# PSUM banks in a 4-2-2 and a 3-2-3 division, in an attention kernel with a fast-product MLP mixer behind it

## The chip, the cores and the metric

The kernel runs on one core of a Trainium2 chip. The metric is the device time of one execution in microseconds (us), as the median of several runs. The core's engines are TensorE (PE), VectorE (DVE), ScalarE (ACT), GpSimd (POOL) and SyncE (SP, which issues most transfers). Each works through its own queue in order. TensorE writes its products into PSUM, which has eight banks; VectorE and ScalarE read them out, which the text calls eviction. A bank can be written again when its last reader is done.

## What is computed

Attention with normalised queries and keys over 8 batches, 12 heads, 448 positions and a head size of 64, and then an MLP mixer (token and channel) on the result, all in float32:

```python
q_n, k_n = (rmsnorm(q, g_q), rmsnorm(k, g_k))
scores = scale * np.matmul(q_n, k_n.transpose(0, 1, 3, 2))
scores = scores - np.max(scores, axis=-1, keepdims=True)
attn = np.exp(scores)
attn = attn / (np.sum(attn, axis=-1, keepdims=True) + 1e-09)
x = np.matmul(attn, v)            # then (B, H, S, D) -> (B, S, H*D)

xt = x.transpose(0, 2, 1)
h = np.maximum(xt @ w_tok1, 0.0) @ w_tok2
u = x + h.transpose(0, 2, 1)
h2 = np.maximum(u @ w_ch1, 0.0) @ w_ch2
out = u + h2
```

The sizes of the mixer are 448 positions, 768 channels, 256 for `w_tok1` and 1536 for `w_ch1`.

## The kernel before

**Overlap of two halves.** The mixer of batch b and the attention of batch b+1 run at the same time: their operations stand interleaved in each engine's queue, in an order that the Python code writes out for TensorE, VectorE, ScalarE and GpSimd (`manual_schedule`). SP's queue is ordered by the framework. From batch 2 on the two channel products of the mixer, `ch1` (line 968) and `ch2` (line 1037), use a fast matrix product: 15 block products in place of 18, whose operands are sums of blocks. Such sums are made on VectorE and GpSimd, and each product is then added into several places, by VectorE, GpSimd and ScalarE, as the tables `C1_STEPS` and `C_STEPS` say. `ch1(b, f, o)` is called 30 times a batch and `ch2(b, f, x)` 30 times; each call is four matmuls, which the profile shows as eight instructions, since a float32 matmul takes two. This text calls such a call a product. A `ch1` call takes a PSUM bank of its own; two `ch2` calls share one.

**Attention.** Pairs of heads are numbered p, and two pairs make a group t. A group has seven key blocks k. `score(t, k)` (line 433) takes two score banks, fills them with four 64x64-tiled matmuls, and ScalarE writes their exponentials into a tile `e`. `values(ps, k)` (line 503) multiplies exponentials by v and adds them up in two output banks (`ps_O`), which are held from k = 0 to k = 6. `group_sums` (line 477) adds exponentials up over k on VectorE, `row_sums` (line 522) sums them over the keys with two products with ones, one for each pair, and `denominators` (line 528) divides: `begin` reads a row-sum bank, `end` multiplies the output bank by the reciprocals (line 560) and so frees it.

**Queries and keys of the next group.** `square` (line 1363, ScalarE) squares them, `reduce` (line 1377, VectorE) sums the squares, `fold` and `guess` prepare a first reciprocal root, three `newton` steps (line 1413, four GpSimd operations each) refine it, `scale` (line 399, VectorE) multiplies, `turn_qk` (line 405) transposes on VectorE and multiplies the queries by the gains on ScalarE. Only then are the buffers free for the loads of the next group. One tile of squares serves both pairs, so `square(n+1)` waits for `reduce(n)`.

**The order around the change.** For batches 2 to 6, `big_step(t, second)` (line 570) makes two TensorE blocks of a group: the first has scores 0 to 2 of this group, values 4 to 6 of the last and its row sums, the second has scores 3 to 6 and values 0 to 3. It returns what runs ahead of the block, the block, what comes directly behind it (`beside`) and a list for the products up to the next block (`between`). Six such blocks, second and first in turn, stand before products 0, 9, 16, 25, 33 and 40 of the 60 (`BLOCKS`, line 1190). `place` (line 620) deals the list out: after the m-th of n products, `upto = -(-len(rest) * (m + 1) // n)` items of it have been emitted (line 627). In earlier batches `att_step` (line 639) makes four smaller steps of a group, merged with the other work by estimated durations.

**PSUM.** Three pools share the eight banks, and each gives its banks out in turn: `ps_S` (4) for scores, row sums, transposes, two of the token products and every other product of `ch1` and `ch2` (`c_ps`), `ps_O` (2) for the values, `ps_M` (2) for the rest (`m_ps`).

Of the kernel before, what the change touches and what calls it, by code (L numbers as in the profile page):

```python
# [110 lines left out]
def whole(ctx, tc, shifted, pre, q, k, v, g_q, g_k, moe_w_tok1, moe_w_tok2, moe_w_ch1, moe_w_ch2, out):  # L111
# [53 lines left out]
    ps_S = pool("ps_S", 4, space=PSUM)  # L165
    ps_O = pool("ps_O", 2, space=PSUM)
    ps_M = pool("ps_M", 2, space=PSUM)
# [354 lines left out]
    def row_sums(t):  # L522
        es = st.pop(("es", t))
        for p in (2 * t, 2 * t + 1):
            st["d", p] = s_tile("d_ps")
            ones(p, es[:, p % 2, :], start=True, stop=True)
# [43 lines left out]
    def big_step(t, second):  # L570
# [68 lines left out]
    def att_step(g):  # L639
# [8 lines left out]
        def finish():  # L648
            if s == 0 and t:
                last = (p - 2, p - 1)  # L650
                for k in (NK - 2, NK - 1):
                    values(last, k)
            if live:
                for k in ((0,), (1, 2), (3, 4), (5, 6))[s]:
                    score(t, k)
            if s == 0 and t:
                if not on_pe(p - 1):
                    row_sums(t - 1)
                for i in last:
                    st.pop(("v", i))  # L660

        def tiled():
# [8 lines left out]
            if inside:  # L671
                for fn in turns:
                    fn()
            if live and s and not shifted:
                for k in ((), (0,), (1, 2), (3, 4))[s]:
                    values(pair, k)
# [291 lines left out]
    def ch1(b, f, o):  # L968

        put_off_done()  # L970
        ps = m_tile() if o else s_tile("c_ps")
# [534 lines left out]
```

## Time and profile before

| | |
|---|---|
| median of 3 runs | 1314.67 us (1314.24 to 1315.56) |
| the profiled execution | 1318.08 us |
| its span, first to last instruction | 1316.2 us |
| granted TensorE clock, mean | 0.992 of full speed |
| DMA traffic | 225.60 MB, mean 171 GB/s |
| TensorE waits put down by name | t_ps for DVE at the start 15.1 us; m_ps of ch2 for DVE 9.4 (5 times); c_ps of ch1 for ACT 3.8 (3 times); m_ps of tok2 for DVE 2.9; c_ps of ch2 for ACT 2.0 (3 times) |

Stages, by TensorE's timeline in us from the span's start: attention of batch 0 from 18 to 81, batch 0's mixer to 258, batch 1's to 427, then batches 2 to 7, which begin at 426.6, 587.7, 741.5, 895.1, 1048.5 and 1196.3. Batch 7 has no attention beside it.

A line of a timeline has the start, the time from the first start to the last end, the engine, the line of the code, the operation, what it writes and reads, the shape and the number of instructions; in brackets stands idle time of the engine ahead of it and what ended it. Matmuls overlap, so their rate is read from the distance of their starts, not from the length of one. A line of a table of windows has the stretch, its length, and for each engine the busy time and the number of instructions, then the granted clock, the busy share of the DMA engines and GB/s.

### The profile page before, as it was taken

The numbers are of one execution on the slowest core, as the hardware profiler recorded it, in microseconds if no ns is written. First come the engines' busy times: TensorE is split into PE (matmuls) and PEld (weight loads), VectorE is DVE, ScalarE is ACT, GpSimd is POOL, SyncE is SP. The second block draws the span as 40 slices with busy tenths as digits, with TensorE's granted clock in tenths as the row PEclk, the third lists the DMA queues.
The fourth block names the chain that finished last, engine by engine and source line by source line (L and its number), as shares of the span: only waits on it lengthen the run. The fifth ranks groups of instructions, "written<-read, shape, count | busy, mean of one in ns | idle before, by whom it ended". The sixth has DMA issues, their size and how long they took to land.

```text
span 1316.2 us, 19628 instructions
## 1 busy us (share of the span) xinstructions
PE 1262.6 (96%) x7048; PEld 871.8 (66%) x7048; DVE 835.9 (64%) x1280; ACT 403.5 (31%) x775; POOL 469.0 (36%) x727
## 2 busy tenths in 40 slices
PE   5999999999999997999999999999999999999996
PEld 3444444444445675696777777786876967797996
DVE  6998769654463566755768368765677557664343
ACT  6663433123320243402443044321434024300210
POOL 1300100079975785430343203450234303430242
PEclk9999999999999999999999999999999999999998
DMA  9666456898888977596567766495765965476664
GB/s 210 172 178 162 120 139 169 203 259 236 234 202 230 212 210 183 114 247 123 115 174 157 191 144 148 115 232 139 167 153 113 252 122 129 122 183 157 177 178 82
DMA packets 480272, 225.60 MB, mean 171 GB/s; under 512 B 375204, under 2 KB 441764, under 8 KB 480164
## 3 DMA queue, kind: packets, MB, share of 16 engines
q1 hardware_dynamic: 462690, 206.68, 65.2%
q0 software_dynamic: 4480, 15.73, 3.9%
q10 hardware_dynamic: 12994, 1.84, 0.9%
q8 instruction: 58, 0.95, 0.3%
q14 instruction: 50, 0.41, 0.1%
HBM read 178.36 MB, written 45.81 MB: 170 GB/s over the span
## 4 chain that ended last, share of the span: by engine, by line
PE 77%; DVE 10%; DMA 4%; SPq 3%; POOL 2%; issue 2%; ACT 2%; DVEq 0%; ACTq 0%; POOLq 0%
PE m_ps L1047 12%; PE c_ps L1047 10%; PE s_ps L441 8%; PE c_ps L979 8%; PE m_ps L979 7%; PE o_ps L514 7%; PE m_ps L862 5%; PE m_ps L1010 4%; PE m_ps L935 4%; PE m_ps L1030 4%; PE t_ps L820 2%; PE m_ps L820 2%; DVE es L482 2%; DMA qk_t<-in_k_dram 2%; DVE hb L1021 1%
## 5 line engine op out<-in xcount | busy, mean ns | idle before, releaser
L445 ACT ACTIVATE e<-s_ps 128x448 f32<-128x448 f32 x294 | 141.4, 556 | 178.9 <-PE s_ps L441 168.9
L441 PE MATMUL s_ps<-qkT 64*64 64x448 f32 x1260 | 169.0, 547 | 2.5 <-DVE r L992 1.7
L1047 PE MATMUL m_ps<-hb,unit 128*128 128x224 f32 x768 | 160.4, 364 | 9.4 <-DVE r L992 9.4
L1047 PEld LDWEIGHTS m_ps<-hb,unit 128*128 128x128 f32 x768 | 150.3, 197 | 12.5 <-DVE r L992 11.1
L295 POOL TENSOR_TENSOR raw<-raw 128x128 f32<-128x128 f32 x256 | 135.2, 549 | 45.8 <-DMA out_dram<-turned 25.5
L514 PE MATMUL o_ps<-e,v 64*64 64x448 f32 x1148 | 144.8, 539 | 0.7 <-DVE uT L560 0.4
L1047 PE MATMUL c_ps<-hb,unit 128*128 128x224 f32 x672 | 135.8, 354 | 2.6 <-ACT e L445 2.0
L1047 PEld LDWEIGHTS c_ps<-hb,unit 128*128 128x128 f32 x672 | 126.3, 190 | 9.9 <-ACT e L445 4.3
L482 DVE TENSOR_TENSOR es<-es,e 128x896 f32<-128x896 f32 x90 | 105.7, 1175 | 14.6 <-ACT e L445 9.6
L441 PEld LDWEIGHTS s_ps<-qkT 64*64 64x64 f32 x1260 | 52.6, 132 | 84.1 <-issue 57.5
L979 PE MATMUL c_ps<-tu,unit 128*128 128x224 f32 x480 | 101.5, 354 | 3.9 <-ACT e L445 3.8
L979 PE MATMUL m_ps<-tu,unit 128*128 128x224 f32 x480 | 102.1, 356 | 1.7 <-DVE hb L992 1.7
L979 PEld LDWEIGHTS m_ps<-tu,unit 128*128 128x128 f32 x480 | 89.7, 190 | 9.9 <-issue 5.6
L979 PEld LDWEIGHTS c_ps<-tu,unit 128*128 128x128 f32 x480 | 90.1, 190 | 9.2 <-ACT e L445 7.6
L514 PEld LDWEIGHTS o_ps<-e,v 64*64 64x64 f32 x1148 | 52.7, 133 | 60.5 <-issue 48.0
L992 POOL TENSOR_TENSOR hb<-hb,r 128x448 f32<-128x448 f32 x36 | 49.5, 1401 | 117.6 <-DVE r L992 80.0
L1062 POOL TENSOR_TENSOR uT<-uT,r 128x448 f32<-128x448 f32 x42 | 52.5, 1262 | 104.0 <-DVE r L1062 92.0
L403 DVE TENSOR_TENSOR qk_t<-qk_t,rs 128x896 f32<-128x896 f32 (+1 forms) x42 | 55.6, 1361 | 43.5 <-POOL rs L1421 43.5
L961 POOL TENSOR_TENSOR tu<-uT 128x448 f32<-128x448 f32 x12 | 13.7, 1139 | 194.2 <-DVE uT L867 117.2
L862 PE MATMUL m_ps<-w_sb,h 128*128 128x448 f32 x192 | 74.4, 541 | 2.9 <-DVE uT L867 2.9
L1418 POOL TENSOR_TENSOR nt<-rs 128x56 f32<-128x56 f32 (+1 forms) x57 | 17.8, 313 | 160.2 <-DVE rs L1410 158.2
L1388 DVE TENSOR_REDUCE ms<-sq 128x28 f32<-128x896 f32 (+2 forms) x44 | 47.4, 1079 | 41.4 <-ACT sq L1374 38.3
(151 smaller groups left out, 1995.5 us busy)
## 6 DMA issues: line engine op xcount, KB each, us to landing
unit<-ws SPq DMA_DIRECT2D x240, 384.0 KB, 3.9
raw<-in_moe_w_ch_dram SPq DMA_DIRECT2D x72, 256.0 KB, 3.4
v<-in_v_dram SPq DMA_DIRECT2D x96, 112.0 KB, 3.9
xs<-xt SPq DMA_DIRECT2D x56, 168.0 KB, 4.5
out_dram<-turned SPq DMA_DIRECT2D x168, 56.0 KB, 2.0
unit<-wp SPq DMA_DIRECT2D x24, 384.0 KB, 4.7
ws<-raw POOLq DMA_DIRECT2D x16, 512.0 KB, 4.9
qk_t<-in_q_dram SPq DMA_DIRECT2D x144, 56.0 KB, 3.5
```

The source lines that it names most:

```text
L295: nc.gpsimd.tensor_tensor(out=at[o], in0=at[x], in1=at[y], op=ALU.add if op == "+" else ALU.subtract)
L403: nc.vector.tensor_tensor(out=x, in0=x, in1=r.unsqueeze(2).to_broadcast(list(x.shape)), op=ALU.mult)
L441: nc.tensor.matmul(out=pss[i][rows_of(i, a), 0:S], lhsT=qkT[h, 1, k * D:(k + 1) * D], rhs=qkT[h, 0, :], start=True, stop=True)
L445: nc.scalar.activation(out=e[:, i, :], in_=pss[i][:, 0:S], func=AF.Exp)
L482: nc.vector.tensor_tensor(out=es[:], in0=(es if k > 1 else st["e", t, 0])[:], in1=st["e", t, k][:], op=ALU.add)
L514: nc.tensor.matmul(out=st["o", p][a * D:(a + 1) * D, 0:S], lhsT=vt[rows, k * D:(k + 1) * D], rhs=e[rows, :], **kw)
L820: nc.tensor.matmul(out=st["t1", h][jc][:, 0:HC], lhsT=w1_sb[:, c, jc * P:(jc + 1) * P], rhs=st["x", b, h][:, :, c, :], start=start and c = ...
L862: nc.tensor.matmul(out=ps[:, 0:S], lhsT=st["h1", jc][:, cc * P:(cc + 1) * P], rhs=w2_sb[:, jc].rearrange("p c r -> p (c r)"), start=(jc == ...
L935: nc.tensor.matmul(out=ps, lhsT=a[:, o + 2 * half, :], rhs=natural(half * KF + t) if wide else u[:, half * KC + t, :], start=(t == 0 and h ...
L979: nc.tensor.matmul(out=ps[:, t * HS:(t + 1) * HS], lhsT=st["w"][:, tile_at % 6, :], rhs=x[:, k, :], start=(k == 0), stop=(k == 1))
L1010: nc.tensor.matmul(out=ps, lhsT=w[:, 3 * o + t, :], rhs=u[:, half * KC + t, :], start=(half == 0 and t == 0), stop=(half == 1 and t == KC ...
L1047: nc.tensor.matmul(out=ps[:, x * HS:(x + 1) * HS], lhsT=st["w"][:, tile_at % 6, :], rhs=hb[:, X_SLOT[f], i, :], start=(i == 0), stop=(i == 3))
```

## The change

The banks are divided 3 for `ps_S`, 2 for `ps_O` and 3 for `ps_M`. All `ch1` and `ch2` products take `ps_M`. In the blocks of `big_step` a value step follows each score step. In `att_step` the two alternate as well, with the transposes of the next queries and keys between them in batch 0's attention, and of the two row-sum banks the first comes from `ps_M`. `reduce(n+1)`, the second sum of squares, moves from directly behind the first block to after the first group sum of the list.

```diff
-    ps_S = pool("ps_S", 4, space=PSUM)
+    ps_S = pool("ps_S", 3, space=PSUM)
     ps_O = pool("ps_O", 2, space=PSUM)
-    ps_M = pool("ps_M", 2, space=PSUM)
+    ps_M = pool("ps_M", 3, space=PSUM)
...
-    def row_sums(t):
+    def row_sums(t, mixed=False):
         es = st.pop(("es", t))
         for p in (2 * t, 2 * t + 1):
-            st["d", p] = s_tile("d_ps")
+            st["d", p] = m_tile() if mixed and p % 2 == 0 else s_tile("d_ps")
             ones(p, es[:, p % 2, :], start=True, stop=True)
...
         def first_block():
-            if live:
-                score(t, 0)
-                score(t, 1)
-            if more and t > BIG:
-                pre.reduce(n, st)
-                pre.square(n + 1, st)
-            for k in range(NK - 2 - (t > BIG), NK):
-                values(last, k)
+            ks = range(NK - 2 - (t > BIG), NK)
+            for i in range(3):
+                if live:
+                    score(t, i)
+                if more and t > BIG and i == 1:
+                    pre.reduce(n, st)
+                    pre.square(n + 1, st)
+                if i < len(ks):
+                    values(last, ks[i])
             row_sums(t - 1)
             for i in last:
                 st.pop(("v", i))
-            if live:
-                score(t, 2)
 
         def second_block():
-            score(t, 3)
-            score(t, 4)
-            for k in range(4):
-                values(pair, k)
-            score(t, 5)
-            score(t, 6)
+            for k, vs in ((3, (0,)), (4, (1, 2)), (5, (3,)), (6, ())):
+                score(t, k)
+                for v in vs:
+                    values(pair, v)
...
-            ahead, beside = (squares[:1], squares[3:]) if t > BIG else ([], [])
+            ahead, beside = squares[:1] if t > BIG else [], []
             between = [item(group_sums, t, k) for k in (1, 2) if live]
+            if t > BIG:
+                between[1:1] = squares[3:]
...
         def finish():
...
+            ks = ((0,), (1, 2), (3, 4), (5, 6))[s] if live else ()
+            vs = ((NK - 2, NK - 1) if t else (), (0,), (1, 2), (3, 4))[s] if s == 0 or live else ()
+            todo = [lambda k=k: score(t, k) for k in ks]
+            of = (p - 2, p - 1) if s == 0 else pair
+            vals = [lambda k=k: values(of, k) for k in vs]
+            order = []
+            while todo or vals:
+                for l in (vals, todo) if s == 0 else (todo, vals):
+                    if l:
+                        order.append(l.pop(0))
+            between = list(turns) if inside else []
+            for fn in order:
+                fn()
+                if between:
+                    between.pop(0)()
+            for fn in between:
+                fn()
             if s == 0 and t:
                 if not on_pe(p - 1):
-                    row_sums(t - 1)
+                    row_sums(t - 1, True)
...
     def ch1(b, f, o):
...
-        ps = m_tile() if o else s_tile("c_ps")
+        ps = m_tile()
...
     def ch2(b, f, x):
...
         if x == 0:
-            st["m"] = s_tile("c_ps") if f % 2 else m_tile()
+            st["m"] = m_tile()
```

More of the change, by code (lines that the diff above doesn't have):

```diff
@@ L648, in finish @@
         def finish():
[L649 to L655, printed above, removed]
+            ks = ((0,), (1, 2), (3, 4), (5, 6))[s] if live else ()
[15 more added lines that the diff above has]
+                fn()
             if s == 0 and t:
                 if not on_pe(p - 1):
-                    row_sums(t - 1)
-                for i in last:
+                    row_sums(t - 1, True)
+                for i in last_pair:
                     st.pop(("v", i))
+        last_pair = (p - 2, p - 1)
         def tiled():
@@ L670, in tiled @@
                     st.pop(("qkT", i))
-            if inside:
+            if inside and shifted:
                 for fn in turns:
                     fn()
-            if live and s and not shifted:
-                for k in ((), (0,), (1, 2), (3, 4))[s]:
-                    values(pair, k)
         def both_shifted():
```

## The prediction

> **What bounds the kernel now.** I read the page first, then TensorE's instructions in order of time, then what VectorE, GpSimd and ScalarE do around TensorE's gaps, and last the granted clock around them.
>
> ```profile
> PE 1262.6 (96%) x7048; PEld 871.8 (66%) x7048; DVE 835.9 (64%) x1280; ACT 403.5 (31%) x775; POOL 469.0 (36%) x727
> ```
>
> TensorE is busy 96% of the span, and the change adds and removes no instruction. So only the gaps in TensorE's stream can pay or cost. I follow batch 4 (741.5 to 895.1 us); batches 3 and 5 repeat it. A to F are its six attention blocks, before mixing products 0, 9, 16, 25, 33 and 40. TensorE's timeline, around block D:
>
> ```profile
> 804.17 1.78 PE L979 MATMUL c_ps<-uT,unit 128*128 128x224 f32 x8
> 805.78 1.68 PE L979 MATMUL m_ps<-uT,unit 128*128 128x224 f32 x8
> 807.30 1.68 PE L979 MATMUL c_ps<-uT,unit 128*128 128x224 f32 x8
> 808.81 1.68 PE L979 MATMUL m_ps<-uT,unit 128*128 128x224 f32 x8
> ...
> 822.00 1.02 PE L494 MATMUL d_ps<-es,one_c 64*64 64x448 f32 x8
> 822.75 1.02 PE L441 MATMUL s_ps<-qkT 64*64 64x448 f32 x8
> 823.70 1.78 PE L979 MATMUL m_ps<-tu,unit 128*128 128x224 f32 x8
> 825.83 1.78 PE L979 MATMUL c_ps<-tu,unit 128*128 128x224 f32 x8 [0.35 <-ACT e L445]
> ```
>
> Starts are 1.51 us apart for a product and 0.75 for one score, value or row-sum step. At these rates a second block (4 scores, 4 values) takes 6.0 us, and a first block (3, 3 and the row sums) 5.3. By the starts on this timeline A takes 6.20, B 6.01, C 7.32, D 5.51, E 7.28 and F 6.14 with the wait behind it: 38.5 where 33.9 is needed, so 4.6 us a batch for the change to win. From the end of D to the end of the first ch2 operation the kernel loses as much again.
>
> **What hides behind the banks now.** The four products above start after block C. VectorE in that time:
>
> ```profile
> 799.90 0.61 DVE L992 TENSOR_TENSOR hb<-hb,m_ps 128x448 f32<-128x448 f32 x1
> 802.56 3.95 DVE L403 TENSOR_TENSOR qk_t<-qk_t,rs 128x896 f32<-128x896 f32 x2 [2.05 <-POOL rs L1421]
> 806.44 1.16 DVE L418 STREAM_TRANSPOSE qkT<-qk_t 128x448 f32<-128x448 f32 x2
> 807.53 2.24 DVE L482 TENSOR_TENSOR es<-es,e 128x896 f32<-128x896 f32 x2
> 809.68 0.61 DVE L992 TENSOR_TENSOR hb<-hb,c_ps 128x448 f32<-128x448 f32 x1
> ```
>
> The first of those products, started at 804.17, is read out of PSUM only from 809.68 to 810.29, behind two scales, two transposes and two group sums. TensorE does not notice: products alternate between two M banks and four S banks, so the fourth starts at 808.81 in a bank of its own. What the scale waits for is on GpSimd:
>
> ```profile
> 800.06 1.13 POOL L992 TENSOR_TENSOR hb<-hb 128x448 f32<-128x448 f32 x1 [2.30 <-DVE hb L992]
> 801.16 0.27 POOL L1418 TENSOR_TENSOR nt<-rs 128x56 f32<-128x56 f32 x1
> ...
> 802.22 0.30 POOL L1421 TENSOR_TENSOR rs<-nt,rs 128x56 f32<-128x56 f32 x1
> ```
>
> The third Newton step (four operations, 1.36 us) stands behind a mixing operation, which waits for VectorE.
>
> **The change, part by part.** *Three banks for all mixing products.* The fourth product after C now needs the bank of the first. *One operation more in the list.* `reduce(n+1)`, one VectorE instruction of 1.09 us with no transfer, leaves the place behind the block (VectorE idle there, from 785.05 to 787.88 after B) and enters the list that is dealt out to the seven products B to C. The list grows from 13 to 14 items. By the rounding of line 627 the shares end at 2, 4, 6, 8, 10, 12, 14 in place of 2, 4, 6, 8, 10, 12, 13: the first product is followed by one group sum and the reduce, `guess` falls from the third product to the fourth, and the first and second Newton steps from the fourth and fifth to the fifth and sixth. Steps two and three then both stand behind that GpSimd mixing operation, one step (1.36) later. VectorE works without a gap from 787.88 to 800.51; it now starts 0.45 earlier (block B, below) and has 1.09 more, so the mixing operation is released 0.64 later. Scale: 802.56 + 1.36 + 0.64 = 804.6. From its start to the end of the first product's eviction took 810.29 - 802.56 = 7.7, so TensorE's fourth product starts at 812.3 instead of 808.81. Six more starts of 1.51 and 0.1 for the change of tile size put D at 821.5 where it was 818.19: **+3.4**. This includes what happens inside C: its second value operand needs an output bank that VectorE frees by its operation on line 560, which ends at 799.45 now and 0.6 later then, so C's own gain lies under a wait that starts earlier.
>
> *The clock.* C then ends near 805.1 (the output bank at 800.1, and 4.9 us of steps left), three products end at 809.6, and TensorE has nothing until 812.3: 2.7 us. Windows of the granted clock (the number after the five engines), around two gaps of before:
>
> ```profile
> 515.50:518.40 2.90, 0.06 (x1) 0.00 (x0) 0.45 (x1) 1.43 (x3) 0.00 (x0) 1.00 1.17 252
> 518.40:521.40 3.00, 2.99 (x16) 2.99 (x17) 2.86 (x5) 1.50 (x3) 0.00 (x0) 1.00 0.68 150
> 832.10:834.10 2.00, 0.05 (x1) 0.00 (x0) 2.00 (x4) 0.00 (x0) 2.00 (x2) 1.00 0.75 197
> 834.10:837.50 3.40, 3.38 (x10) 3.06 (x11) 3.30 (x7) 0.76 (x1) 3.40 (x4) 0.54 0.17 66
> ```
>
> A gap of 2.8 us left the clock at 1.00, one of 2.0 was followed by 3.4 us at about half, and the 16 instructions after it took 4.98 where others take about 3.1: 1.9 more. So a new gap costs 0 to 1.9 beyond itself; I take the middle, **+0.95**.
>
> [...]
>
> *Three score banks, scores and values in turn.* Exponentials take about 0.46 each in a row (1.85 for four). In B, by 0.75 us steps, every score finds its bank free: it loses its wait for mixing banks, **-0.45** (in the sum above already). In E a ch2 operation no longer holds an S bank across the block: between nothing and -1.26; VectorE's line 560 is late here as well, so **-0.8**. A has nothing to win. The last row sum of a first block, however, now takes the bank of score 2, and so waits for an exponential that stands behind `square(n+1)` on ScalarE:
>
> ```profile
> 824.39 0.95 ACT L1374 ACTIVATE sq<-qk_t 128x896 f32<-128x896 f32 x1 [3.25 <-DMA qk_t<-in_k_dram]
> 825.25 0.96 ACT L445 ACTIVATE e<-s_ps 128x448 f32<-128x448 f32 x2
> ```
>
> In D the square waits for a transfer until 6.2 us after the block's start. The row sum, ready at 4.9, goes at about 7.6, with all mixing products queued behind it on TensorE. Today one product runs before that wait. The VectorE chain to ch2 starts 1.7 later, but the first evictions and a group sum no longer stand behind the late reduce. Adding the operations up from TensorE's 826.3 (evictions 0.62 each, sums and forms 1.1) the first ch2 product starts near 835.9, 1.8 later than now, and may save the 1.9 of slow clock there: 0 to +1.5, **+0.5**. In F the square ends 5.6 after the start and the next product goes at 6.6 where it went at 6.14: **+0.5**. SP's order is not written out by the kernel; q, k and v transfers may move by a product, which I put at nothing, between -1 and +1 in a batch.
>
> *The beginning.* Score pairs at 58.42 and 68.20 take 2.59 and 2.32 to the next operation where 1.5 would do: alternating saves 0 to 3, I take **-2**. A third M bank shortens tok2's 2.9 us of waits for VectorE (0 to -2.9): **-1**.
>
> **The sum.** Batches 3 to 5: 3.4 + 0.95 + 0.5 - 0.8 + 0.5 = 4.55 each, 13.7. Batch 6 has no square in D and no scores in F: 3.4 + 0.95 - 0.8, 3.5. Batch 2 is already held by GpSimd (block D comes 1.9 later by the same steps, of which its late square hides some): 2.5. With -3 at the beginning: +16.7. The profiled execution took 1318.08 (span 1316.2 and 1.9 around it), so 1334.8; the median shown is 3.4 less, so **1331**. With every bound at its good end +2 (1317), with every one at its bad end +33 (1348); its likely part is 1320 to 1341.
>
> **Rivals.** *The change wins.* Score waits go (3.6 of the 4.6 us a batch, A to F) and VectorE no longer stops at the late reduce. The wait of 825.83 for an exponential speaks for it, and 4.7 us of VectorE's time before the late reduce in D. Five batches of 3.6 make 18: 1297. It decides from the point where the first product's eviction after C ends before the third product does. That needs the scale by 803.05 + 4.54 - 7.73 = 799.9, and VectorE is full until 800.5 and GpSimd until 802.5 today. Chance 0.13. *The banks wait, but the list's shift is harmless* (the Newton steps find their gap): the fourth product at 810.3, +1.5 in place of 3.4 and no slow clock; with the other terms about 1.2 a batch, less 3 at the beginning: 1318, chance 0.12. *Each wait also halves the clock*, in C and in D: 1.9 twice a batch, over 1341 and near 1345: 0.08. *Alternating does nothing,* since waits on ScalarE only move within a block: the -0.8 goes, 1335, inside my forecast. My forecast has 0.62; something between winning and 1318 that cannot be told from the time before has 0.05.
>
> A difference under 0.2% (2.6 us) is not told from no change here. Faster 0.14 (the first rival and a little of the last), same 0.06, slower 0.80. The range 1311 to 1341 leaves about 0.11 below and 0.09 above.
>
> **What would show it.** In the new trace, seven products after each B, block C, then three products and a gap of 2 to 4 us before the fourth, put down to VectorE's eviction on line 992 (batches 2 to 6); the scale's wait for GpSimd grown from 2.05 to about 4; row sums in D waiting for ScalarE's exponential; no score waiting for a mixing eviction. The forecast is wrong if the fourth product after C starts without a gap, or if TensorE's idle time falls.

## The result, and the profile after

| | before | after |
|---|---|---|
| median of 4 runs each, same chip | 1314.45 us (1312.58 to 1315.56) | 1352.26 us (1350.34 to 1353.52) |
| ratio, 95% interval | | 1.0288 [1.0269, 1.0306] |
| profiled execution, and its span | 1318.08, 1316.2 us | 1353.21, 1351.4 us |
| granted TensorE clock, mean | 0.992 | 0.993 |

The change makes the kernel 37.8 us slower. The forecast was 16.7 slower on the profiled execution, 1331 as a median, with a range that ended at 1341. The direction was right, the size was less than half. Below, lines of the code are numbered as in the changed kernel: behind `att_step` they are 8 higher than before (992 is 1000, 1047 is 1055, 979 is 987). Rows of a kernel of the experiments have that kernel's own numbers.

First the page's row of busy times after the change:

```profile
PE 1275.8 (94%) x7048; PEld 879.8 (65%) x7048; DVE 837.5 (62%) x1280; ACT 411.7 (30%) x775; POOL 468.2 (35%) x727
```

The instruction counts are those of before, and VectorE, ScalarE and GpSimd have hardly more work (1.6 and 8.2 us more, 0.8 less). TensorE, with the same instructions, is busy 13.2 us longer, and idle for the other 22.0 of the 35.2 us by which the span grew. The waits of TensorE by name (tile and line that wait, engine and tile that end the wait, us in total, times, longest):

```profile
PE t_ps L415 <- DVE g_t L1182: 15.3, 1, 15.3
PE m_ps L987 <- DVE hb L1000: 10.9, 5, 2.3
PE o_ps L514 <- DVE uT L560: 8.7, 13, 1.2
PE m_ps L1055 <- DVE r L1000: 8.3, 5, 1.7
PE d_ps L494 <- ACT e L445: 7.2, 6, 3.8
PE d_ps L494 <- ACT cv_sb L445: 3.4, 2, 2.8
PE s_ps L441 <- ACT e L445: 3.1, 2, 1.6
```

The start's 15.3 us and the ch2 wait (8.3, was 9.4) are old. Three groups are new: a ch1 product waits for VectorE's eviction once in each of five batches (10.9), values wait for output banks (8.7, was 0.4), and row sums wait for exponentials (7.2 and 3.4).

Where the time went, by stage (distances between the first token product of one batch and that of the next, from TensorE's timelines; us):

| stage | before | after | difference | forecast |
|---|---|---|---|---|
| up to batch 0's mixer | 80.87 | 83.91 | +3.0 | -3 |
| batch 0 | 177.26 | 179.16 | +1.9 | 0 |
| batch 1 | 168.45 | 173.36 | +4.9 | 0 |
| batch 2 | 161.16 | 169.86 | +8.7 | +2.5 |
| batch 3 | 153.76 | 158.20 | +4.4 | +4.55 |
| batch 4 | 153.63 | 158.32 | +4.7 | +4.55 |
| batch 5 | 153.39 | 158.37 | +5.0 | +4.55 |
| batch 6 | 147.82 | 150.13 | +2.3 | +3.5 |

A batch 0 of about 179 is also found in two kernels below that change nothing there (reduce_only 179.2, four_merged 179.5), so its +1.9 is within what one profile differs from the next.

TensorE around block C of batch 4, the place that the forecast worked out (start, time from first start to last end, engine, line, operation, tiles, shape, count; idle time and its end in brackets):

```profile
822.41 0.59 PE L514 MATMUL o_ps<-cv_sb,v 64*64 64x448 f32 x2 [0.89 <-DVE uT L560]
...
826.61 1.28 PE L441 MATMUL s_ps<-qkT 64*64 64x448 f32 x6
827.83 4.81 PE L987 MATMUL m_ps<-uT,unit 128*128 128x224 f32 x24
834.77 1.78 PE L987 MATMUL m_ps<-uT,unit 128*128 128x224 f32 x8 [2.13 <-DVE hb L1000]
836.38 7.81 PE L987 MATMUL m_ps<-tu,unit 128*128 128x224 f32 x40
```

Three products (24 instructions) start at 827.83 and fill the three product banks; the fourth starts only at 834.77, when VectorE has read the first. VectorE and GpSimd in that time:

```profile
822.27 1.14 DVE L1000 TENSOR_TENSOR hb<-hb,m_ps 128x448 f32<-128x448 f32 x2
826.98 3.95 DVE L403 TENSOR_TENSOR qk_t<-qk_t,rs 128x896 f32<-128x896 f32 x2 [3.56 <-POOL rs L1429]
830.85 1.16 DVE L418 STREAM_TRANSPOSE qkT<-qk_t 128x448 f32<-128x448 f32 x2
831.94 2.24 DVE L482 TENSOR_TENSOR es<-es,e 128x896 f32<-128x896 f32 x2
834.10 0.61 DVE L1000 TENSOR_TENSOR hb<-hb,m_ps 128x448 f32<-128x448 f32 x1
```

```profile
823.03 1.14 POOL L1000 TENSOR_TENSOR hb<-hb 128x448 f32<-128x448 f32 x1 [2.77 <-DVE hb L1000]
824.13 0.28 POOL L1426 TENSOR_TENSOR nt<-rs 128x56 f32<-128x56 f32 x1
825.20 0.30 POOL L1429 TENSOR_TENSOR rs<-nt,rs 128x56 f32<-128x56 f32 x1
825.58 0.28 POOL L1426 TENSOR_TENSOR nt<-rs 128x56 f32<-128x56 f32 x1
826.65 0.30 POOL L1429 TENSOR_TENSOR rs<-nt,rs 128x56 f32<-128x56 f32 x1
```

Two Newton steps (824.13 to 825.50 and 825.58 to 826.95) now stand behind the mixing operation of 823.03 where one stood before. The scale's wait has grown from 2.05 to 3.56, and the eviction that frees the first bank ends at 834.71, with TensorE going on at 834.77. The clock in this gap and after it (windows: stretch, length, busy time of PE, PEld, DVE, ACT and POOL, then the granted clock):

```profile
832.60:834.77 2.17, 0.04 (x2) 0.01 (x1) 2.07 (x4) 0.11 (x1) 0.00 (x0) 1.00 0.66 109
834.77:838.20 3.43, 3.43 (x18) 3.27 (x19) 3.43 (x6) 1.54 (x3) 0.00 (x0) 1.00 0.94 239
...
861.60:865.00 3.40, 3.39 (x18) 3.39 (x19) 3.29 (x7) 0.78 (x1) 3.40 (x4) 1.00 0.17 66
```

It stayed at 1.00, and the third stretch, in which ch2 begins, ran at 1.00 too, where before it was 0.54. Not every batch is like that. Here are the 3.41 us in which the gap of batch 4 mostly lies and the 3.41 us behind them, then the same for batch 5, whose gap is as long (2.12):

```profile
832.89:836.30 3.41, 1.53 (x8) 1.43 (x8) 3.31 (x7) 0.47 (x1) 0.00 (x0) 1.00 0.72 141
836.30:839.71 3.41, 3.41 (x20) 3.36 (x19) 3.15 (x4) 1.60 (x4) 0.93 (x1) 1.00 1.04 247
989.90:993.31 3.41, 1.29 (x7) 0.94 (x6) 3.31 (x5) 0.67 (x1) 0.00 (x0) 1.00 0.51 83
993.31:996.72 3.41, 3.41 (x11) 3.08 (x11) 2.34 (x6) 1.51 (x2) 0.00 (x0) 0.50 0.97 261
```

Until its last products the changed kernel has four such stretches at 0.50, each 3.41 us long: three in batch 2 (from 484.73, 512.03 and 532.51) and this one. The kernel before has four as well, one at the start of ch2 in each of batches 2 to 5. Block B of batch 2, the stage with the largest loss, holds its row sums up (the first row), and block D, on TensorE and on ScalarE, does so for longer:

```profile
483.36 0.97 PE L494 MATMUL d_ps<-es,one_c 64*64 64x448 f32 x4 [2.79 <-ACT cv_sb L445]
...
527.99 0.54 PE L494 MATMUL d_ps<-es,one_c 64*64 64x448 f32 x2
532.33 1.62 PE L494 MATMUL d_ps<-es,one_c 64*64 64x448 f32 x4 [3.80 <-ACT e L445]
533.88 2.40 PE L987 MATMUL m_ps<-tu,unit 128*128 128x224 f32 x6
```

```profile
525.63 0.98 ACT L445 ACTIVATE e<-s_ps 128x448 f32<-128x448 f32 x2 [0.20 <-PE s_ps L441]
530.89 0.95 ACT L1382 ACTIVATE sq<-qk_t 128x896 f32<-128x896 f32 x1 [4.29 <-DMA qk_t<-in_k_dram]
531.75 0.96 ACT L445 ACTIVATE e<-s_ps 128x448 f32<-128x448 f32 x2
```

In D `square(n+1)` waits 4.29 us for its transfer; the third score's exponentials wait behind it until 531.75; the second row sum needs the bank that the first of them frees, and starts at 532.33; all mixing products stand behind the row sum. Last, block E of batch 4, on TensorE and VectorE:

```profile
866.35 0.98 PE L441 MATMUL s_ps<-qkT 64*64 64x448 f32 x8
868.08 0.97 PE L514 MATMUL o_ps<-e,v 64*64 64x448 f32 x4 [0.75 <-DVE uT L560]
869.29 0.59 PE L514 MATMUL o_ps<-e,v 64*64 64x448 f32 x2 [0.24 <-DVE uT L560]
```

```profile
867.40 0.62 DVE L560 TENSOR_TENSOR uT<-o_ps,rd 128x448 f32<-128x448 f32 x1
868.61 0.62 DVE L560 TENSOR_TENSOR uT<-o_ps,rd 128x448 f32<-128x448 f32 x1
```

The first values now wait 0.75 us behind the first score, and the two normalisations that free their output banks end at 868.02 and 869.23.

### The profile page after: what moved, and what is told of

Same layout as the page of the kernel before. It is cut to its first block, busy times and chain, and to the rows that moved or that the text cites. A ratio compares the mean times of both kernels' runs of the same rounds, so it can differ in the third digit from the quotient of the medians.

```text
span 1351.4 us, 19662 instructions
## 1 busy us (share of the span) xinstructions
PE 1275.8 (94%) x7048; PEld 879.8 (65%) x7048; DVE 837.5 (62%) x1280; ACT 411.7 (30%) x775; POOL 468.2 (35%) x727
## 4 chain that ended last, share of the span: by engine, by line
PE 76%; DVE 13%; issue 3%; DMA 3%; SPq 2%; ACT 2%; POOL 1%; DVEq 0%; ACTq 0%; POOLq 0%
PE m_ps L1055 19%; PE m_ps L987 15%; PE s_ps L441 8%; PE o_ps L514 7%; PE m_ps L870 5%; PE m_ps L1018 4%; PE m_ps L1038 4%; PE m_ps L943 4%; PE m_ps L828 2%; PE t_ps L828 2%; DVE es L482 2%; DVE hb L1000 2%; PE m_ps L494 1%; PE d_ps L494 1%; DMA qk_t<-in_k_dram 1%
## 5 line engine op out<-in xcount | busy, mean ns | idle before, releaser
L1055 PE MATMUL m_ps<-hb,unit 128*128 128x224 f32 x1440 | 276.6, 354 | 8.3 <-DVE r L1000 8.3
L1055 PEld LDWEIGHTS m_ps<-hb,unit 128*128 128x128 f32 x1440 | 271.2, 190 | 17.1 <-DVE r L1000 10.0
L445 ACT ACTIVATE e<-s_ps 128x448 f32<-128x448 f32 x294 | 146.7, 542 | 169.9 <-PE s_ps L441 166.4
L987 PE MATMUL m_ps<-tu,unit 128*128 128x224 f32 x960 | 192.6, 358 | 1.7 <-DVE r L1000 1.7
L987 PEld LDWEIGHTS m_ps<-tu,unit 128*128 128x128 f32 x960 | 182.1, 192 | 15.6 <-issue 11.6
L514 PE MATMUL o_ps<-e,v 64*64 64x448 f32 x1148 | 168.4, 540 | 8.1 <-DVE uT L560 6.8
L482 DVE TENSOR_TENSOR es<-es,e 128x896 f32<-128x896 f32 x90 | 101.2, 1124 | 13.9 <-ACT e L445 10.9
L987 PE MATMUL m_ps<-uT,unit 128*128 128x224 f32 x480 | 99.1, 363 | 10.9 <-DVE hb L1000 10.9
L987 PEld LDWEIGHTS m_ps<-uT,unit 128*128 128x128 f32 x480 | 92.6, 195 | 16.7 <-DVE hb L1000 12.6
L1000 DVE TENSOR_TENSOR r<-r,m_ps 128x448 f32<-128x448 f32 x36 | 22.2, 618 | 93.2 <-PE m_ps L987 93.2
L875 DVE TENSOR_TENSOR uT<-uT,m_ps 128x448 f32<-128x448 f32 x48 | 29.6, 619 | 67.6 <-PE m_ps L870 67.6
L1000 POOL TENSOR_TENSOR hb<-hb 128x448 f32<-128x448 f32 x24 | 35.4, 1476 | 90.1 <-DVE hb L1000 90.1
```

Of the source, the lines that this page charges most:

```text
L445: nc.scalar.activation(out=e[:, i, :], in_=pss[i][:, 0:S], func=AF.Exp)
L482: nc.vector.tensor_tensor(out=es[:], in0=(es if k > 1 else st["e", t, 0])[:], in1=st["e", t, k][:], op=ALU.add)
L514: nc.tensor.matmul(out=st["o", p][a * D:(a + 1) * D, 0:S], lhsT=vt[rows, k * D:(k + 1) * D], rhs=e[rows, :], **kw)
L987: nc.tensor.matmul(out=ps[:, t * HS:(t + 1) * HS], lhsT=st["w"][:, tile_at % 6, :], rhs=x[:, k, :], start=(k == 0), stop=(k == 1))
L1000: e.tensor_tensor(out=at[out], in0=at[a], in1=at[c], op=ALU.add if op == "+" else ALU.subtract)
L1055: nc.tensor.matmul(out=ps[:, x * HS:(x + 1) * HS], lhsT=st["w"][:, tile_at % 6, :], rhs=hb[:, X_SLOT[f], i, :], start=(i == 0), stop=(i == 3))
```

## The experiments

Eighteen kernels, in five groups; ratios are to the kernel before on the same chip, with a 95% interval. "Wait" is a row of TensorE's waits. Differences in us between two of the kernels are of their medians, which come from different chips (the kernel before took 1314.5 to 1317.7 there): where the intervals of the two ratios overlap, the difference is not clear.

### Parts of the change alone

**banks_only**: the 3-2-3 division alone.

```diff
-    ps_S = pool("ps_S", 4, space=PSUM)
+    ps_S = pool("ps_S", 3, space=PSUM)
-    ps_M = pool("ps_M", 2, space=PSUM)
+    ps_M = pool("ps_M", 3, space=PSUM)
-        ps = m_tile() if o else s_tile("c_ps")
+        ps = m_tile()
-            st["m"] = s_tile("c_ps") if f % 2 else m_tile()
+            st["m"] = m_tile()
```

> The kernel before with the banks divided 3-2-3 and all ch1 and ch2 products in ps_M; scores, values and the reduce stand as before. If too few banks for the products are the main cost, TensorE waits for VectorE's eviction (line 992) at the fourth product after block C in batches 2 to 6, about 1.5 us each, and score pairs lose some 0.5 us a step to three score banks: 1320 to 1335 us. If alternating is the main cost, this is within 5 us of before (1314). If the reduce's place is, the same.

Measured: 1372.79 us, 1.041 [1.0353, 1.0467]. Its waits:

```profile
PE s_ps L441 <- ACT e L445: 18.1, 21, 2.6
PE t_ps L415 <- DVE g_t L1174: 15.3, 1, 15.3
PE m_ps L979 <- DVE hb L992: 7.4, 5, 2.9
```

The division alone loses more than the whole change. Two scores in a row want four banks; with three, the second one's last matmuls wait for the first one's exponentials, 21 times, where before that row was 0.4 in one wait. Neither time that was expected is near this.

**turn_only**: scores and values alternate, in long and short steps; 4-2-2 banks, reduce in its old place (the change's diff of `first_block`, `second_block` and `finish`, with no `True` for `row_sums`).

> The kernel before with scores and values in turn in big_step and att_step alone; banks 4-2-2, reduce in its old place. If the banks are the main cost, this is 1308 to 1320 us, with no wait of a product for its bank beyond those of before. If alternating itself costs (value step 0 comes a score earlier and finds its output banks not yet free; a score or a value is the last of a block where it was not), TensorE waits for VectorE's line 560 and ScalarE's line 551 several times and the time is 1322 to 1335.

Measured: 1317.65, 0.9996 [0.9971, 1.002]. With four score banks alternation is worth nothing.

**reduce_only**: the kernel before, the reduce as an item of the list.

```diff
-            ahead, beside = (squares[:1], squares[3:]) if t > BIG else ([], [])
+            ahead, beside = squares[:1] if t > BIG else [], []
...
+            if t > BIG:
+                between[1:1] = squares[3:]
```

> The kernel before with the second sum of squares after the first group sum alone. If the longer list pushes two Newton steps behind a mixing operation of GpSimd, the scale after block C starts about 2 us later in batches 2 to 6; with five to six banks in turn TensorE feels part of it: 1314 to 1325 us. If its merit (VectorE no longer stops for a late square in block D) is the larger, the product at the border of ch1 and ch2 starts earlier and the time is 1302 to 1312.

Measured: 1320.0, 1.0018 [0.9995, 1.0041]: no clear difference.

**after_reduce_back**: the changed kernel without this edit.

> The changed kernel with the reduce directly behind the block again. If the list's shift is what makes the fourth product after C late, its wait of 2.1 us goes to nearly 0 and the time falls by 5 to 12 us to 1340 to 1347. If three banks are too few in any case, the wait stays above 1.5 us and the time is within 3 us of 1352; if the reduce's place was a merit, it grows.

Measured: 1342.26, 1.0166 [1.0107, 1.0225], 10 us less than the changed kernel by the medians, 9.2 by the spans of the two profiles; batches 3 to 6 take 155.5, 155.0, 153.7 and 148.4, batch 2 still 171.4. Block E of batch 4 takes 6.33 us in place of 8.36. The reduce's new place is a loss where all products share the three banks, but hardly one where every other product has a score bank.

### Order in the long steps

**after_square**: the changed kernel, with `square(n+1)` behind the third score.

```diff
-                if more and t > BIG and i == 1:
-                    pre.reduce(n, st)
-                    pre.square(n + 1, st)
+                if more and t > BIG and i == 1:
+                    pre.reduce(n, st)
                 if i < len(ks):
                     values(last, ks[i])
+            if more and t > BIG:
+                pre.square(n + 1, st)
             row_sums(t - 1)
```

> The changed kernel with one call moved: in the first block of a long step, square(n+1) is issued after the third score instead of after the second. Theory A: part of the loss is order on ScalarE and VectorE. The square waits for its load, the exponentials of the third score stand behind it, and with three score banks the row sums find no bank (waits of 7.2 us on ScalarE's e and 3.4 us on cv_sb in front of the row sums, 7.2 of it in batch 2). Then these 10.6 us go nearly whole: about 1343 us, batch 2 some 6 us shorter, batches 3 to 6 about 1 us each. Theory B: the row sums wait because three banks hold two scores' exponentials whatever stands ahead of them; then the wait stays and the time is 1349 to 1355.

Measured: 1336.24, 1.0164 [1.014, 1.0188]: 16 us less from one moved call, more than theory A had. Batch 2 falls from 169.9 to 158.0. Rows of `d_ps` are gone, the others stand:

```profile
PE m_ps L988 <- DVE hb L1001: 10.9, 5, 2.4
PE m_ps L1056 <- DVE r L1001: 8.3, 5, 1.7
PE o_ps L514 <- DVE uT L560: 8.1, 13, 0.9
```

**after_sums**: the changed kernel, with group sums 3 and 4 moved from `beside` to the head of the second block's list.

> The changed kernel with the group sums 3 and 4 of a long step moved from right behind the second block into the list that is dealt out over the following products. Theory A: VectorE works in order, and the first eviction after the second block stands behind scale, transposes and these sums, so that the fourth product waits for a bank once in each of batches 2 to 6 (10.9 us in five waits, 2.1 to 2.3 each). With two sums (about 1.3 us together) out of the way the wait falls to about 1 us: 4 to 9 us less, 1343 to 1348. Theory B: the sums only change places, exponential buffers come free later and the next block's scores or the evictions further back wait instead: 1350 to 1356.

Measured: 1348.38, 1.0256 [1.0234, 1.0279], 3.9 less. The product's wait fell from 10.9 to 6.0, but 3.8 us more of score waits came (s_ps on e 5.1, on cv_sb 1.8). Some of both theories: the two sums are a part of what stands ahead of the eviction, and what they free comes later. The intervals overlap, so whether the time is less is not clear.

**after_values_late**: values one place later in the second block.

```diff
-            for k, vs in ((3, (0,)), (4, (1, 2)), (5, (3,)), (6, ())):
+            for k, vs in ((3, ()), (4, (0,)), (5, (1, 2)), (6, (3,))):
```

> The changed kernel with the values of the second long block one place later (s3 s4 v0 s5 v1 v2 s6 v3). Theory A: the first values wait for the value banks that VectorE's normalization frees late (o_ps on uT: 8.7 us in 13 waits); 1.5 us later the wait is mostly gone: 1344 to 1348. Theory B: two scores in a row again stand before three score banks, and the fifth score waits for the fourth's exponentials instead (s_ps on e grows from 3.1 to 8 or more): 1350 to 1358.

Measured: 1355.19, 1.0296 [1.0261, 1.0331], not clearly different from the changed kernel. The wait for output banks fell from 8.7 to 0.7, while s_ps on e grew to 5.9 and the ch1 product's wait to 14.7. The 8.7 us are there, but a later value only hands them on.

### Banks or order?

**after_att_back**: the changed kernel with the short steps of `att_step` in the old order.

> The changed kernel with the short attention steps (beginning, batches 0 and 1) in the old order, the scores first and then the values; the long steps still alternate. Theory A: alternation itself costs the short steps 0.1 us each and some bank waits; undone, beginning to batch 1 are 3 to 6 us shorter, 1346 to 1349 in all. Theory B: with three score banks, two scores in a row stand waiting for the exponentials, as in the kernel with the banks alone (88.5 us to the first batch, 184.5 and 179.5 in batches 0 and 1, against 83.9, 179.2 and 173.4 in the changed kernel): 8 to 15 us longer, 1360 to 1367.

Measured: 1361.49, 1.0361 [1.033, 1.0391], 9 more. The beginning takes 89.9 in place of 83.9, batch 0 181.9, batch 1 176.1 (the beginning has one stretch at half clock, which the changed kernel has not, worth about 1.7 us by an estimate from its 3.41 us). So alternation is no loss in the short steps, it saves some of what the three score banks cost there (theory B).

**after_4_2**: the changed kernel with four score and two product banks, the products still all in product banks, row sums in score banks.

> The changed kernel with 4-2-2 banks, but all products of the mixing in the two product banks as in the changed kernel (none goes through the score banks), and the row sums in score banks. Theory A: the products need three banks to run ahead of their evictions; with two, every product waits for the eviction of the one before the last: far slower than the changed kernel, 1375 to 1420, with the waits on VectorE's and ScalarE's evictions in the five mixed batches. Theory B: what costs is the fourth score bank that is gone; then the row sums' and scores' waits go and the time is 1325 to 1340.

Measured: 1338.2, 1.0183 [1.016, 1.0206]: theory B's time, but with the waits of theory A:

```profile
PE m_ps L987 <- DVE hb L1000: 21.9, 14, 3.3
PE m_ps L987 <- DVE r L1000: 17.3, 11, 1.9
```

Beginning, batch 0 and batch 1 are back at 80.8, 178.2 and 167.9, and batch 2 at 157.3: what the early stages and batch 2 lost, they lost to the division. Batches 3 to 6 take 160.3, 157.6, 156.3 and 153.5: with two banks the products wait 39 us for VectorE. (Batch 3 also holds 13.7 us at half clock here.) The third product bank is worth something, but only to the products, and no row of `o_ps` on VectorE is left (8.7 in the changed kernel): where products wait earlier, VectorE is less behind at the values.

**after_rows_m**: the changed kernel with the first row sum of a long step in a product bank (`row_sums(t - 1, True)` in `first_block`).

> The changed kernel with the first row sum of a long step in a product bank (as the short steps have it); the square stays after the second score. Theory A: the row sums wait because the second of them takes the bank that the third score's exponential, behind the late square, has not read yet; the first row sum no longer takes a score bank, so a score bank is free for the second one: the waits of the row sums (7.2 and 3.4 us) shrink to under 3, and with them batch 2: 1339 to 1345. Theory B: the late square holds the chain anyway, through its reduce; the next product then waits for a product bank that VectorE or the row sum holds: 1348 to 1356.

Measured: 1337.32, 1.0142 [1.0111, 1.0172], 15 less, a little beyond theory A. The square is where the change left it, and the rows of `d_ps` are gone all the same; batch 2 takes 158.2. The row sum waited for a score bank. (A later wait of products for r grew from 1.7 to 17.3 in ten waits.)

### Why the reduce costs

**after_square_back**: after_square with the reduce back in `beside`.

> The changed kernel with both earlier edits: square(n+1) after the third score, and the reduce back in its old place behind the first block. Theory A: the late square costs through the row sums' wait for a score bank, the reduce through VectorE's and POOL's order in the products; the two are independent, so 16 and 10 us add up: 1324 to 1329, batch 2 about 158, batches 3 to 5 about 153. Theory B: both act on the same wait (with the reduce back the waits of the row sums were still 11.2 and 4.2 us, which the square takes away, but then the block begins earlier and meets the next late work): 1332 to 1337.

Measured: 1320.32, 1.0044 [1.0027, 1.0061]. From the changed kernel 32 us by the medians, 6 more than the two edits make singly; by the ratios 2.4 points, just the sum of 1.2 and 1.2. In the profiles, where the excess is 6.8 us, most of it is the clock: until the last products the changed kernel, after_square and after_reduce_back each have 13.65 us at half clock, and this kernel has 3.41, which makes about 5 us (an estimate, half of the difference). Batches 3 to 5 take 152.2, 151.9 and 151.7, which is 1.6 to 1.8 *under* the kernel before. That too is the clock: they have no stretch at half clock, and the kernel before has one of 3.41 us in each, while TensorE's idle time is not less (3.6, 3.6 and 3.5 us in them, before 3.2, 3.0 and 2.8). What is left of the loss is in the beginning (83.6) and batch 1 (171.7).

**after_square_merged**: after_square, the reduce at its new place, but as one list item with the first group sum: 13 items, not 14.

```diff
-                between[1:1] = squares[3:]
+                between[:1] = [(0.8, lambda fns=(between[0], *squares[3:]): [fn() for _, fn in fns])] if live else squares[3:]
```

> The changed kernel with square(n+1) after the third score (1336.2 us) and the reduce at its new place, but as one item of the list with the first group sum: the list has 13 items as in the kernel before, and guess and Newton steps stand beside the same products as there. Theory A: the reduce's new place costs because the fourteenth item shifts what follows it, so that Newton steps stand behind GpSimd's mixing operations; without the shift most of the 16 us come back: 1320 to 1327, the wait of the fourth product (m_ps for hb, 10.9 us) falls to about 6. Theory B: the cost is the 1.09 us on VectorE in front of the group sum and the later start of the Newton chain: 1332 to 1338.

Measured: 1322.05, 1.0023 [1.0007, 1.004], 14 less than after_square. VectorE has the reduce at the same place; what follows it in the list, `guess` and the Newton steps among it, goes back to its products. TensorE after block C of batch 4, and VectorE's scale there:

```profile
809.77 4.81 PE L988 MATMUL m_ps<-uT,unit 128*128 128x224 f32 x24
815.18 1.78 PE L988 MATMUL m_ps<-uT,unit 128*128 128x224 f32 x8 [0.61 <-DVE hb L1001]
...
807.40 3.95 DVE L403 TENSOR_TENSOR qk_t<-qk_t,rs 128x896 f32<-128x896 f32 x2 [2.05 <-POOL rs L1430]
```

The wait for the bank is 0.61 in place of 2.14, and over the batches 3.7 in place of 10.9; the scale waits 2.05 as in the kernel before, in place of 3.57. Block E of batch 3 takes 6.33 in place of 8.36. The list's shift was the cost. About half of the 14 us is the clock: after_square has a stretch of 3.41 us at half clock behind this gap in batches 2, 3, 5 and 6, and this kernel has none until its last products (about 6.8 us, an estimate).

**square_back_turn_m**: after_square_back with the TensorE transposes of `turn_qk` in a product bank.

> The changed kernel with the square after the third score and the reduce back (1320.3 us), and the TensorE transposes of queries and keys (for the first two batches' attention) in a product bank in place of a score bank. Theory A: beginning to batch 1 lose time because transposes, row sums and scores share three banks; 1 to 4 us less: 1316 to 1319. Theory B: the product banks hold the row sums of batch 0's attention for seven steps, so the one free bank makes the transposes wait for each other: 1321 to 1330.

Measured: 1326.02, 1.006 [1.0042, 1.0077], worse by 5.7 by the medians and by 2 by the ratios, whose intervals overlap; the profiles speak for theory B: batch 0 takes 183.2 (178.9 in after_square_back), batch 1 174.1 (171.7). The rest of the early loss isn't to be had by this.

### The parts at 4-2-2

**square_only**: the kernel before, `square(n+1)` at the end of the first block.

> The kernel before with one call moved: square(n+1) at the end of the first block, after the third score. Theory A: with four score banks the late square is covered, since a bank is free for the row sums and the next product whatever the exponentials do; only the waits of c_ps on ScalarE's e (3.8 and 2.0 us) shrink: 1311 to 1316. Theory B: the late square costs four banks as much as three: 1300 to 1306, batch 2 near 155.

Measured: 1324.34, 1.0073 [1.0046, 1.01]: slower, which neither theory had. The wait of ch2's first product for VectorE grew from 9.4 to 16.0. In the old order the third score comes last in the block, so that the square starts only after the row sums, and the reduce behind the block still stands ahead of the first evictions. In batch 3 VectorE waits for the square until 674.87, and the reduce then keeps the eviction of the product that started at 672.00 until 675.87. TensorE pays at ch2's first product (1.98 us before, now 3.70):

```profile
678.16 1.68 PE L980 MATMUL m_ps<-tu,unit 128*128 128x224 f32 x8
683.54 4.98 PE L1048 MATMUL m_ps<-hb,unit 128*128 128x224 f32 x16 [3.70 <-DVE r L993]
```

**long_turn**: the kernel before with `first_block` and `second_block` alternating, nothing else.

> The kernel before with nothing but scores and values alternating in the long steps (4-2-2, reduce and square in the old place, short steps in the old order). Theory A: the gain of batches 4 to 6 (1.9, 2.4 and 1.0 us in the run that alternated everywhere) stands alone, since the short steps lost what it won: 1307 to 1311. Theory B: alternation is worth nothing with four score banks: 1313 to 1317.

Measured: 1317.12, 0.9996 [0.9977, 1.0015]. Nothing: batches 5 and 6 win 2.4 and 1.0, batch 2 loses 2.5.

**long_turn_square**: long_turn with the square behind the third score.

> The kernel before (4-2-2 banks, reduce in its old place, short steps in the old order) with the long steps alternating and square(n+1) after the third score. Theory A: alternation in the long steps gave 1 to 2.5 us in each of batches 4 to 6 at 4-2-2 but its early stages lost as much; without the short steps' change the gain stands, and the earlier exponentials add to it: 1304 to 1311. Theory B: what alternation gains is given back in the next products, and the time is that of the kernel before: 1313 to 1318.

Measured: 1312.45, 0.9974 [0.9956, 0.9993], a small gain between the two theories. Alternating, the third score comes earlier in the block, and with it the square (in block B of batch 3 4.97 us after the block's start, in square_only 6.56). That this turns the loss of square_only into a gain is likely, but not shown: in block D of batch 4 the square waits for its transfer and is no earlier (7.12 against 6.45).

**four_merged** and **four_square_merged**: the last two with the reduce as one list item with the first group sum.

> The same with square(n+1) in its old place after the second score. Theory A: the late square costs waits of c_ps for ScalarE's e (6.0, 2.6, 2.5 and 2.4 us with the alternation alone), which stay, but the reduce in the list is no loss: 1310 to 1316. Theory B: the reduce is late anyway for the square's transfer and in the list it stops the evictions behind it: 1317 to 1325.

> 4-2-2 banks, every other product of the mixing in a score bank, short steps in the old order; the long steps alternate, square(n+1) comes after the third score, and the reduce is one item of the list with the first group sum. Theory A: with the late square alone a ch2 product waited for VectorE up to 5.2 us, since the reduce behind the block keeps the evictions waiting for the square; in the list it doesn't, the wait (14.6 us in five) falls to about 7, and the time is 1303 to 1309, under both kernels. Theory B: GpSimd's Newton steps start later and the scale with them, so the wait moves: 1312 to 1320.

Measured: four_merged 1313.99, 0.9962 [0.9943, 0.9981]; four_square_merged 1308.78, 0.9926 [0.9904, 0.9947]. The latter beats both kernels. Batches 2 to 6 take 156.2, 152.0, 151.7, 152.0 and 146.9. The c_ps products' waits for exponentials (6.0, 2.6, 2.5 and 2.4 us in long_turn) no longer stand among its waits, and ch2's wait for VectorE is 12.1, under the 14.6 of long_turn_square but not the 7 that theory A wanted, though the time is as it said:

```profile
PE m_ps L1047 <- DVE r L992: 12.1, 5, 2.8
```

## Why the prediction was right in sign and wrong in size

**The fourth product after C: right.** Seven products, block C, three products and a gap for VectorE's eviction came as written: 2.13 us (forecast 2.7), the scale's wait 3.56 (forecast about 4). From A's to D's start batch 4 takes 2.9 more (forecast 3.4, where its own figures, 818.19 and 821.5, make 3.3). after_square_merged shows its cause, the list's shift: without it 14 us come back, and the rival "the list's shift is harmless" falls with that. It was harmless where the products have score banks as well (reduce_only).

**The clock: 0 in batch 4, not +0.95, and not the same in every batch.** Of the five gaps after C (2.12 to 2.35 us) those of batches 2 and 5 were followed by 3.41 us at 0.50, those of 3, 4 and 6 were not. In batch 5 it costs 1.6 (the nine products after C take 17.89, in batch 4 16.29), so 0.4 as the mean of batches 3 to 6.

**Block E: +1.1 in batches 3 to 5, not -0.8.** The forecast saw that line 560 is late, and still booked a gain. Alternation puts the first values behind one score in place of two, 0.75 us earlier, and so onto that late operation (0.75 and 0.24 us of waits). What makes it too late is the list's shift, which the forecast followed only as far as C: with the reduce back behind the block (after_reduce_back) or tied to its neighbour (after_square_merged) block E takes 6.33, nearly 1 us less than before, and the gain is there. after_values_late shows that it can't be had by moving the values back.

**D to E and F: about right.** -0.1 for +0.5, and +0.8 for +0.5. Counted from D's start, ch2 begins 1.6 later (forecast 1.8), and its first products run at full clock, which saves 1.7 (forecast 0 to 1.9). That batches 3 to 5 take 4.4 to 5.0 more, against 4.55, is in part luck: the miss in E cancels those in the clock, in D and in the fourth product.

**The step that failed: three score banks, in the stages that were not worked out.** The forecast priced the missing score bank in batch 4 alone and carried its numbers over; even its sum with every bound at its bad end (1348) stays under what was measured. For batch 2 it let the late square *hide* some of the loss (+2.5). The opposite holds: there the square is latest, and the row sum, with all products behind it, waits 2.79 us in B and 3.80 in D. The two blocks take 3.2 and 2.8 us more than before, of the batch's loss of 8.7, and behind these two waits and the gap after C the clock fell to 0.50 for 3.41 us, three times where it fell once before. after_square and after_rows_m each take this away, one from the square's side and one from the bank's, and both end at 158 for batch 2. For the beginning the forecast had -3 (alternation -2, token products -1) and for batch 1 nothing; they were +3.0 and +4.9. (The token products' wait for VectorE did fall, from 2.9 to 0.6, but it lies in batch 0, which is no shorter.) The forecast's premise that only TensorE's gaps can cost fails here as well: 7.3 of these 7.9 us are busy time of TensorE, by the same instructions at a granted clock of 1.00. Alternation was not a gain there but the repair of the new loss: 6 us of it in the beginning (after_att_back) and none with four banks (turn_only: 81.6). after_4_2 brings both stages back to those of before. Beginning, batch 1 and batch 2 are 6.0, 4.9 and 6.2 of the miss of 21 us; batch 0 is 1.9 (not above noise), and 2.4 is the distance of the profiled execution to the median, 3.4 before and 1.0 after; the other batches together are -0.7.

**The rivals.** "The change wins" needed the first eviction before the third product; it came 2.1 us after it. "Each wait also halves the clock" came true in batch 2 (in B, after C and in D) and after C in batch 5, and not in batches 3, 4 and 6. "Alternating does nothing" is true at 4-2-2 (0.9996 twice), and false at 3-2-3, where the division without it costs 1372.8 and with it 1342.3 (banks_only against after_reduce_back, which also has a row sum of the short steps in a product bank). The 1318 of "the list's shift is harmless" is, by other sums than its own, about what the change comes to once shift and square are mended: 1322.1 and 1320.3.

**What stays open.** Of the early loss only waits of 1.3 us (beginning) and 1.6 us (batch 1) stand under a name; the rest is spread over the short steps as busy time, and no run here says whether it is the score tiles or the transposes that lack the bank. after_4_2 shows that the division causes it, not how.

## What to carry to other kernels

A PSUM bank was not worth the same in every pool (1352.3 us in the changed kernel, 1338.2 in after_4_2, where the scores have the bank and the products lack it): count for each pool how many tiles its consumer holds at the latest moment of the schedule, and price the loss in every stage, above all in the one where a transfer is late: there an order that four banks covered set the time with three (batch 2: 169.9 us, 157.3 in after_4_2). An operation that enters a list which is dealt out by count shifts all that follows it, up to blocks far behind (E here); tied to its neighbour it cost hardly more than in its old place (1322 and 1320, where as an item of its own it was 1336). Read the clock in every stage, not in one: about half of a difference was stretches at half clock here (6.8 of 14 us, an estimate). Where a division of banks loses, test its order parts at the old division: here two moved calls and the alternation made 0.7% there.

## What the runs showed of the hardware that was not expected

An idle gap of TensorE of 2.13 us (batch 4) left the granted clock at 1.00, where one of 2.12 in batch 5 of the same kernel and one of 1.97 in batch 4 of the kernel before were each followed by 3.41 us at half clock: in these runs the length of the gap alone doesn't say whether the clock falls. The two traces show what stood ahead of each such stretch, up to the last products. Before, the four start at 527.16, 680.76, 834.36 and 987.96 us, and in the 3.41 us ahead of each TensorE was busy for 1.43 to 1.44. After, they start at 484.73, 512.03, 532.51 and 993.31, with 1.37, 1.21, 0.18 and 1.29 us busy ahead of them; in batch 4, where the clock stayed, the 3.41 us in which the gap mostly lies have 1.53. What decides between the two was not shown. Batches 3 to 5 of the kernel before take 153.4 to 153.8 us each, and each has one such stretch.
